# Issuing the transpose and the store of a query block's maxima one step later in a four-layer attention kernel

## The chip, the cores and the metric

The kernel runs on one core of one Trainium2 chip. The metric is the device time of one execution in microseconds (us). The engines are TensorE (PE for its matmuls, PEld for its weight loads), VectorE (DVE), ScalarE (ACT), GpSimd (POOL) and SyncE (SP), which issues every DMA of this kernel.

## The reference

Four residual layers, A, B, A, B, on x of 2048 tokens by 576 features, float32. Each layer normalizes x, does attention with 32 heads of 18 features and adds the projected result. In A every head has its own keys and values; in B all heads share one set.

```python
def _A_ref(x, wqkv, wo):
    qkv = (lambda x, *d: x.transpose(*d))((x @ wqkv).reshape(B, S, 3, H, Dh), 2, 0, 3, 1, 4)
    q, k, v = qkv[0], qkv[1], qkv[2]
    scores = jnp.einsum("bhqd,bhkd->bhqk", q, k) * (Dh ** -0.5)
    p = _softmax(scores, axis=-1)
    o = jnp.einsum("bhqk,bhkd->bhqd", p, v)
    return (lambda x, *d: x.transpose(*d))(o, 0, 2, 1, 3).reshape(B, S, D) @ wo
x = A_x
x = x + _A_ref(_layernorm(x, axis=-1), A_wqkv, A_wo)
x = x + _B_ref(_layernorm(x, axis=-1), B_wq, B_wk, B_wv, B_wo)
x = x + _A_ref(_layernorm(x, axis=-1), A_wqkv, A_wo)
x = x + _B_ref(_layernorm(x, axis=-1), B_wq, B_wk, B_wv, B_wo)
```

## The kernel before

Each layer projects q, k and v, then runs attention, then projects the output. Attention is cut into units: 16 pairs of heads `p` times 4 query blocks `u` of 512 queries, 64 units a layer and 256 in all. The two heads of a pair sit in the two row halves of TensorE, so two score matmuls can run side by side.

The scores of a unit are computed twice. The **max pass** (`max_mm`) lays queries on partitions: 32 tiles `psm` of 128 queries by 512 keys, each reduced to one maximum per query by VectorE (L615). For eight key blocks a difference tile `psd` goes through a Relu on ScalarE (L605) and is added to another tile before the maximum is taken (L612, the kinds `d` and `t`), which saves VectorE four tiles. The **exp pass** (`exp_mm`, L756) lays keys on partitions: 32 tiles `pse` of 128 keys by 512 queries, which ScalarE turns into `pt` or `side` (L762). `pv_block` (L783) multiplies these by the values into `oacc`. The `psm` tiles rotate through three PSUM banks, the `pse` and `psd` tiles through four, so a matmul waits until the reduction or the exponential of the tile three or four places before it has been read.

The maximum reaches the exponential through the matmul. When the 32nd max tile of a unit is reduced, `max_final` (L730) takes the negated maximum per query (`neg`, L732, VectorE) and splits it on GpSimd into a high and a low part (`hl`, L197 and L736). `max_store` (L738) transposes `hl` on VectorE (`tr`, L741) and issues four small DMAs that write it to DRAM (`m_d`, L743). `max_rows` (L745) issues two DMAs that read it back into two rows of the query operand `big` (L747), which face rows of ones in the keys. `exp_mm` of that unit reads these rows.

The order of the work is written out by hand. `UNIT` lists, for the two halves, `e` (an exp tile), `m`, `t` or `d` (a max tile); a number is so many columns of `pv_block`. While the exp tiles of one unit run, the max tiles of later ones run in between. The 32nd max tile of the next unit falls on the ninth word of the list.

```python
UNIT = """te ee 256 em me 384 et em me 512 et me ee 448 md dm em 384 em me 192 me ee me 192 md em 384
          me me em 384 em ee te 192 mm ee 384 dm em em 384 me"""
```

Everything else is hung on steps. A step is four exp tiles, a unit has `STEPS` = 8 of them, and `run_todo` is called before every word of the list with `LEAD + STEPS * w + sum(e_next) // 4`; it emits what is due. Instructions go to each engine's queue in the order in which they are emitted, and each queue is worked off in that order.

```python
b = STEPS * (4 * p + u) + STEPS - 1
if is_a or p or u:
    at(b + NM_AT, max_store, p, u)
    at(b + ROW_AT, max_rows, p, u)
for d, f in ((SUM_AT, o_sum), (L_AT, l_part), (INV_AT, l_inv), (R_AT, l_out), (RB_AT, l_rows),
             (MUL_AT, o_mul), (O_AT, o_out)):
    at(b + LEAD + d, f, p, u)
```

Counted from the start of the unit whose exp tiles run (w), the steps hold: step 2 `l_rows` of unit w-2; step 3 `o_sum` of w-1 and `max_store` of w+1; step 4 `o_mul` of w-2 and `l_part` of w-1, and in one unit of four `load_kd`; step 6 `o_out` of w-2 and `max_rows` of w+1; step 7 `l_inv` and `l_out` of w-1. Within a step the order is that of the calls of `at`, an earlier unit's before a later one's, `load_kd` last. `o_sum` and `o_mul` are GpSimd work on the sums (`os`, L197, L797, L819); `l_part` (L802), `l_out` (L809), `l_rows` (L814), `o_out` (L824) and `load_kd` (L486) issue DMAs.

Of the kernel before, what the change touches and what calls it, by code (L numbers as in the profile page):

```python
# [43 lines left out]

STEPS = 8
LEAD = 14
NM_AT = 2
ROW_AT = 5
SUM_AT = 4
L_AT = 5  # L50
# [72 lines left out]
def tile_kernel(ctx: ExitStack, tc: tile.TileContext, A_x, A_wqkv, A_wo, B_x, B_wq, B_wk, B_wv, B_wo, out):  # L123
# [291 lines left out]
    for layer in range(4):  # L415
# [412 lines left out]
        def at(b, f, *args):  # L828
            todo.setdefault(b, []).append((f, args))

        ns = STEPS * 4 * NPAIR
        for p in range(NPAIR):
            for u in range(4):
# [4 lines that stand above are left out]
# [93 lines left out]
```

## Time and profile before

| | before |
|---|---|
| median of 3 runs | 5737.49 us (5735.5 to 5739.29) |
| the profiled execution | 5738.74 us |
| its span | 5736.9 us |
| granted TensorE clock | 0.999 |
| units' distance in the steady part of a layer | 19.02 us |

The span runs from the first to the last instruction; the profiled execution's own time is 1.8 us more. An engine's busy time is the union of its instructions. TensorE's matmuls are pipelined and overlap, so its 99% is not 99% of what it could do; whether it waits is read from the starts of neighbouring matmuls. In the lists of instructions, a row gives the start in us from the span's start, the time from its first start to its last end, engine, line, operation, output and inputs, and how many were merged; in brackets stands the idle time before it and what ended that.

### The profile page before, as it was taken

How to read it: one execution, taken by the hardware profiler on the slowest of the kernel's cores; microseconds unless marked ns; L12 is line 12 of the kernel's file. 1: busy time of each engine (PE TensorE's matmuls, PEld its weight loads, DVE VectorE, ACT ScalarE, POOL GpSimd, SP SyncE). 2: the span in 40 equal slices, each digit the busy share in tenths (PEclk: the TensorE clock that was granted, in tenths of full speed). 3: DMA queues.
4: the chain of work that ended last, by engine and by line, in shares of the span. 5: the costliest groups of instructions: out<-in, count | busy, mean ns of one | idle time of the engine just before them, and what ended most of it. 6: DMA issues, size and time to landing. Idle time of an engine off the chain costs nothing.

```text
span 5736.9 us, 139041 instructions
## 1 busy us (share of the span) xinstructions
PE 5672.8 (99%) x53724; PEld 2800.5 (49%) x53724; DVE 4941.0 (86%) x9513; ACT 4951.8 (86%) x9868; POOL 1741.0 (30%) x2236
## 2 busy tenths in 40 slices
PE   9999999999999999999999999999999999999999
PEld 7644444444844444444685444444448444444446
DVE  5699999998699999999647999999977999999995
ACT  2599999999389999999625999999992899999996
POOL 3142323234233233333421332323342323323232
PEclk9999999999999999999999999999999999999999
DMA  6311111111320010000253111111114100000002
GB/s 224 114 45 38 35 38 35 38 36 25 125 67 23 23 23 20 22 21 24 59 191 94 49 36 37 38 36 39 33 31 134 53 23 24 23 23 20 23 14 78
DMA packets 258560, 291.64 MB, mean 51 GB/s; under 512 B 132700, under 2 KB 172892, under 8 KB 248176
## 3 DMA queue, kind: packets, MB, share of 16 engines
q1 hardware_dynamic: 257896, 282.75, 17.5%
q8 instruction: 422, 6.91, 0.5%
q14 instruction: 242, 1.98, 0.1%
HBM read 158.77 MB, written 119.86 MB: 49 GB/s over the span
## 4 chain that ended last, share of the span: by engine, by line
PE 74%; DVE 21%; POOL 2%; issue 1%; ACT 1%; DMA 0%; POOLq 0%; SPq 0%; DVEq 0%; ACTq 0%
PE oacc L783 26%; PE psm L608 18%; PE pse L756 16%; DVE mxd L615 13%; PE psn L275 6%; PE psq L434 6%; DVE side L612 6%; PE psd L600 2%; DVE tr L741 1%; POOL hl L736 1%; DVE neg L732 1%; POOL hl L197 1%; DVE mx L615 1%; PE ps L267 0%; POOLq L197 0%
## 5 line engine op out<-in xcount | busy, mean ns | idle before, releaser
L615 DVE TENSOR_REDUCE mxd<-psm 128x1 f32<-128x512 f32 x5856 | 3645.1, 681 | 129.8 <-PE pse L756 46.6
L762 ACT ACTIVATE pt<-pse 128x512 f32<-128x512 f32 x6580 | 3588.3, 622 | 110.6 <-PE pse L756 58.7
L608 PE MATMUL psm<-big 62*128 62x512 f32 x7216 | 2619.9, 453 | 30.6 <-DVE mx L615 5.0
L756 PE MATMUL pse<-big 64*128 64x512 f32 x8192 | 2465.5, 434 | 4.4 <-ACT pt L762 2.7
L783 PE MATMUL oacc<-pt,vbuf 128*19 128x64 f32 (+6 forms) x20492 | 1797.6, 377 | 3.8 <-DVE oc L197 3.6
L756 PEld LDWEIGHTS pse<-big 64*128 64x128 f32 x8192 | 1213.1, 185 | 904.8 <-ACT pt L762 538.3
L608 PEld LDWEIGHTS psm<-big 62*128 62x128 f32 x7216 | 1147.6, 184 | 807.4 <-DVE mxd L615 427.6
L783 PE MATMUL oacc<-side,vbuf 128*19 128x64 f32 (+6 forms) x5044 | 1408.5, 376 | 6.8 <-ACT side L762 6.8
L762 ACT ACTIVATE side<-pse 128x512 f32<-128x512 f32 x1612 | 999.9, 620 | 18.7 <-PE pse L756 7.1
L197 POOL TENSOR_SCALAR hl<-neg 128x8 fp32r<-128x8 f32 x256 | 50.6, 197 | 2854.6 <-DVE neg L732 2854.6
L783 PEld LDWEIGHTS oacc<-pt,vbuf 128*19 128x19 f32 x20492 | 454.2, 97 | 618.2 <-issue 504.7
L612 DVE CUSTOM_DVE_ANT_0 side<-psm,side 128x512 f32<-128x512 f32 x976 | 668.9, 685 | 36.5 <-PE psm L608 10.7
L605 ACT ACTIVATE side<-psd 128x512 f32<-128x512 f32 x976 | 591.6, 649 | 0.0
L783 PE MATMUL oacc<-pt,vy 128*19 128x384 f32 (+3 forms) x5756 | 587.6, 415 | 0.0
L806 POOL TENSOR_TENSOR rl<-lt,mone 128x8 f32<-128x8 f32 x256 | 422.9, 1652 | 358.2 <-DMA lt<-os 358.2
L783 PE MATMUL oacc<-side,vy 128*19 128x384 f32 (+2 forms) x1412 | 456.0, 414 | 0.0
L600 PE MATMUL psd<-kd,big 54*128 54x512 f32 x976 | 420.5, 471 | 0.0
L783 PEld LDWEIGHTS oacc<-side,vbuf 128*19 128x19 f32 x5044 | 319.8, 97 | 157.3 <-issue 124.6
L442 ACT ACTIVATE ev<-psq 128x512 fp32r<-128x512 f32 (+1 forms) x112 | 66.9, 598 | 325.9 <-PE psq L434 272.4
L819 POOL TENSOR_TENSOR os<-os,rb 96x512 f32<-96x512 f32 x256 | 327.7, 1280 | 20.6 <-DMA rb<-r_d 20.6
L797 POOL TENSOR_TENSOR os<-os,side 96x512 f32<-96x512 f32 x240 | 306.5, 1277 | 20.0
L197 POOL TENSOR_SCALAR os<-side 32x512 f32<-32x512 f32 x480 | 293.6, 612 | 40.0 <-POOL hl L736 0.2
(93 smaller groups left out, 3407.4 us busy)
## 6 DMA issues: line engine op xcount, KB each, us to landing
big<-qk_d SPq DMA_DIRECT2D x180, 432.0 KB
qk_d<-ev SPq DMA_DIRECT2D x96, 512.0 KB
qk_d<-ev SPq DMA_DIRECT2D x120, 256.0 KB
rb<-r_d SPq DMA_DIRECT2D x512, 36.0 KB
o_d<-os SPq DMA_DIRECT2D x512, 36.0 KB
m_d<-tr SPq DMA_DIRECT2D x1024, 2.0 KB
o<-o_d SPq DMA_DIRECT2D x64, 256.0 KB
big<-m_d SPq DMA_DIRECT2D x512, 4.0 KB
```

Of the source, the lines that this page charges most:

```text
L197: eng.tensor_scalar(dst, src, 1.0, 0.0, op0=OP.mult, op1=OP.add)
L275: nc.tensor.matmul(ps, lhs[:, xc, :], wsm[:, wc, h * 288:(h + 1) * 288], start=i == 0, stop=i == len(TERMS) - 1)
L434: nc.tensor.matmul(ps[:n].rearrange("p (u t) -> p u t", u=2)[:, us], w[:, wc, :n], xts[T][:, us, xc, :], start=(xc, wc) == TERMS[0], stop= ...
L600: nc.tensor.matmul(ps, q[b:b + 3 * DH, c0:c0 + P], kds[p if is_a else 0][b:b + 3 * DH], start=True, stop=True)
L605: nc.scalar.activation(r, ps, AF.Relu)
L608: nc.tensor.matmul(ps, q[b:b + KM, c0:c0 + P], k[b:b + KM, kb * 512:(kb + 1) * 512], start=True, stop=True)
L612: nc.vector.tensor_tensor_reduce(out=r, in0=ps, in1=r, scale=1.0, scalar=-3.0e38, op0=OP.add, op1=OP.max, accum_out=mx[:, r0:r0 + 1])
L615: nc.vector.reduce_max(mx[:, r0:r0 + 1], ps, axis=AX.X)
L756: nc.tensor.matmul(e, k[r:r + KE, kc * P:(kc + 1) * P], q[r:r + KE, u * 512:(u + 1) * 512], start=True, stop=True)
L762: nc.scalar.activation(pt, e, AF.Exp, scale=SCALE)
L783: nc.tensor.matmul(oacc[j:j + DH + 1, cs], v_of(kc)[:, 2 * p + a if is_a else 0, :], pts[p, u, i][:, cs], start=kc < 2 and c0 == 0, stop=k ...
L806: nc.gpsimd.tensor_tensor(rl, lts.pop((p, u)), mone, op=OP.pow)
```

## The change

`NM_AT` goes from 2 to 3. `max_store` of unit w+1 is emitted at step 4 of unit w where it was emitted at step 3. On VectorE the transpose then stands behind the reductions of the six max tiles in the words `md dm em em me me` (one of each word, `d` tiles go to ScalarE); on SP its four DMAs stand behind the two of `l_part`. `max_rows` stays at step 6. No instruction is added, removed or resized.

```diff
 STEPS = 8
 LEAD = 14
-NM_AT = 2
+NM_AT = 3
 ROW_AT = 5
 SUM_AT = 4
 L_AT = 5
```

## The prediction

> **What bounds the kernel now.** First the page: totals and the chain that ended last.
>
> ```profile
> span 5736.9 us, 139041 instructions
> ...
> PE 5672.8 (99%) x53724; PEld 2800.5 (49%) x53724; DVE 4941.0 (86%) x9513; ACT 4951.8 (86%) x9868; POOL 1741.0 (30%) x2236
> ...
> PE 74%; DVE 21%; POOL 2%; issue 1%; ACT 1%; DMA 0%; POOLq 0%; SPq 0%; DVEq 0%; ACTq 0%
> ```
>
> The chain lies on TensorE for three quarters and on VectorE for a fifth. GpSimd's 2% is odd for an engine that is idle 70% of the time: a GpSimd instruction is passed on the way. The list of waits says where, and the view of tile `tr` how often and how regularly the instruction runs.
>
> ```profile
> DVE tr L741 <- POOL hl L736: 152.4, 252, 0.6
> ...
> L741 DVE STREAM_TRANSPOSE tr<-hl x256: 200/211/215, 205.7 to 5644.3; 128x32 f32<-128x32 f32 x128
> ```
>
> In 252 of 256 units VectorE stands still for 152.4 / 252 = 0.605 us in front of the transpose until GpSimd has split the maxima. Whether that costs time is read from one unit: the chain in order of time, then VectorE's own list, around 804 us.
>
> ```profile
> 804.38 0.21 DVE tr L741
> 804.59 1.18 DVE mxd L615 x2
> 805.77 0.04 issue
> 805.81 0.49 PE psm L608
> ...
> 822.61 0.20 DVE neg L732
> ```
>
> ```profile
> 803.58 0.19 DVE L732 TENSOR_REDUCE neg<-mxd 128x8 f32<-128x32 f32 x1
> 804.38 0.21 DVE L741 STREAM_TRANSPOSE tr<-hl 128x32 f32<-128x32 f32 x1 [0.61 <-POOL hl L736]
> 804.51 5.43 DVE L615 TENSOR_REDUCE mxd<-psm 128x1 f32<-128x512 f32 x9
> 810.14 2.48 DVE L615 TENSOR_REDUCE mxd<-psm 128x1 f32<-128x512 f32 x4 [0.20 <-PE pse L756]
> ```
>
> The unit is 822.61 - 803.58 = 19.03 us long. The chain goes through the transpose and two reductions to the matmul at 805.81, and from there stays on TensorE until the next unit's reductions. After the transpose VectorE runs nine reductions without a break, 5.43 / 9 = 0.60 us each, and then waits again for TensorE. So it is late for a third of the unit only. TensorE's list tells what that costs; the first three rows are a place where it doesn't wait.
>
> ```profile
> 798.36 0.49 PE L756 MATMUL pse<-big 64*128 64x512 f32 x1
> ...
> 798.70 0.40 PE L756 MATMUL pse<-big 64*128 64x512 f32 x1
> 799.03 0.51 PE L783 MATMUL oacc<-pt,vy 128*19 128x384 f32 x3
> ...
> 803.45 0.50 PE L608 MATMUL psm<-big 62*128 62x512 f32 x1
> ...
> 805.20 0.50 PE L756 MATMUL pse<-big 64*128 64x512 f32 x1
> ...
> 805.81 0.49 PE L756 MATMUL pse<-big 64*128 64x512 f32 x1
> 806.24 0.34 PE L783 MATMUL oacc<-pt,vbuf 128*19 128x192 f32 x1
> ...
> 805.81 0.18 PEld L608 LDWEIGHTS psm<-big 62*128 62x128 f32 x1 [0.41 <-DVE mxd L615]
> ```
>
> Unhindered, a second pair of score matmuls starts 798.70 - 798.36 = 0.34 us after the first, and the value matmuls 799.03 - 798.70 = 0.33 us after that. Here it is 805.81 - 805.20 = 0.61 and 806.24 - 805.81 = 0.43. The weight load at 805.81 was let go by a reduction (that of the second tile after the transpose). So VectorE's lateness costs TensorE 0.61 - 0.34 = 0.27 us, and 0.10 us more because a weight load that waits can't run ahead: **0.37 us a unit**, not the 0.605 that VectorE stands.
>
> **The change part by part.** *VectorE's stall goes.* After `neg` the next instruction is now a reduction. Its tile is ready at 803.45 + 0.50 = 803.95; before, it started at 804.51. It can start up to 0.56 us earlier, and the second reduction, whose end lets the matmul go, with it: 805.77 - 0.56 = 805.21 at the earliest. TensorE wants that bank at 805.20 + 0.34 = 805.54, so it no longer waits as long as 0.23 of the 0.56 us are won. I take the whole 0.37.
>
> *The transpose at its new place.* Six reductions of 0.60 us after about 804.0 put it near 807.6. GpSimd's split was ready for the old place at 804.38, so nothing is waited for. It takes 804.51 - 804.38 = 0.13 us of VectorE's order. Just behind lies the 0.20 us idle time at 810.14, where VectorE waits for TensorE: the cover. VectorE itself runs 0.56 - 0.37 = 0.19 us further ahead of TensorE than now, so 0.20 + 0.19 - 0.13 leaves 0.26 us. I take nothing. Without the cover it would be 0.13 us x 252 = 33 us.
>
> *ScalarE.* It must follow a TensorE that is 0.37 us earlier.
>
> ```profile
> 804.27 1.14 ACT L605 ACTIVATE side<-psd 128x512 f32<-128x512 f32 x2
> ...
> 806.38 0.60 ACT L762 ACTIVATE side<-pse 128x512 f32<-128x512 f32 x1
> 807.26 2.06 ACT L762 ACTIVATE pt<-pse 128x512 f32<-128x512 f32 x4 [0.29 <-PE psm L608]
> ...
> 803.58:822.61 19.03, 18.93 (x194) 8.22 (x196) 17.70 (x34) 18.65 (x38) 5.79 (x7) 1.00 0.17 46
> ```
>
> The exponential at 806.38 started when its matmul ended (805.81 + 0.49 = 806.30), and the next one after 0.29 us of idle time, so ScalarE is waiting for the very matmuls that come earlier; it follows. But the last row (busy times of one unit: PE, PEld, DVE, ACT, POOL) leaves ScalarE only 19.03 - 18.65 = 0.38 us without any instruction. Overlap of neighbours makes that look tighter than it is: two L605 at 804.27 take 1.14 us together, four L762 at 807.26 take 2.06, so one more costs (2.06 - 1.14) / 2 = 0.46 us, and 37 tiles (32 exponentials, four Relu, one copy of `oacc`) cost 37 x 0.46 = 17.0 us. From both ends the reserve is 0.38 to 2.0 us; 0.37 fits into either. I cost it at nothing.
>
> *The DMAs.* SP's list of the same unit, then GpSimd's, then the first matmul that reads the rows:
>
> ```profile
> 804.62 1.69 SPq L743 DMA_DIRECT2D m_d<-tr  x4
> 807.12 1.14 SPq L802 DMA_DIRECT2D lt<-os  x2
> 808.37 0.80 SPq L486 DMA_DIRECT2D kd<-kd_d  x2
> 809.26 1.72 SPq L824 DMA_DIRECT2D o_d<-os  x2
> 811.08 0.54 SPq L747 DMA_DIRECT2D big<-m_d  x2
> 811.71 0.56 SPq L809 DMA_DIRECT2D r_d<-rl  x1
> ...
> 813.99 0.63 SPq L814 DMA_DIRECT2D rb<-r_d  x2
> ...
> 804.43 1.30 POOL L197 TENSOR_SCALAR os<-side 32x512 f32<-32x512 f32 x2
> ...
> 807.06 1.28 POOL L819 TENSOR_TENSOR os<-os,rb 96x512 f32<-96x512 f32 x1
> ...
> 816.17 0.71 PE L756 MATMUL pse<-big 64*128 64x512 f32 x3
> ```
>
> The four stores move from 804.62 behind `lt`: 807.12 + 1.14 = 808.3 (the transpose is done by 807.9). They end at 808.3 + 1.69 = 810.0. Behind them on SP come `kd` (one unit in four), `o_d` and the rows: 810.0 + 0.8 + 1.7 = 812.5. The rows also need the stores' data in DRAM. No row gives a landing; the nearest is the write `r_d`, issued by 811.71 + 0.56 = 812.27, whose reader `rb` starts at 813.99: 1.7 us. That gives 811.7, earlier than the queue. Rows issued by 812.5 + 0.54 = 813.1 and landed, with the same 1.7 us, at 814.8; lower end, with no landing time at all, 813.1. The first matmul that reads them is the three merged at 816.17, then at 815.80. Reserve: 1.0 to 2.7 us in this unit, which has all five issues, and 0.8 more where `kd` is missing. `r_d`, `rb` and the value sums behind them start 1.5 us later in the same way; `rb` is used by L819 in the next unit, at 807.06 + 19.03 = 826.1, ten us after its landing. I cost the queue at nothing.
>
> [...]
>
> *Sum.* 0.37 us x 252 units = 93 us. The profiled execution took 1.8 us beyond its span, 5738.7 us, and 1.25 us more than the median; 5737.5 - 93 = **5644 us**. Bounds of this case: only the wait itself, 0.27 us, is 68 us (5669); everything by which VectorE can come forward, 0.56 us, is 141 us (5596).
>
> **The rivals.** *VectorE's whole stall comes back* (a longer gain): 252 x 0.605 = 152 us, 5585 us. It would need further TensorE waits that come from the same lateness; the chain shows none after 805.81, which speaks against it.
>
> *ScalarE takes part of it back*: if its smallest reserve (0.38 us, all of it at the places where it is idle now) is used up by its own order, the unit shortens by about half of 0.37, say 0.18 us: 45 us, 5692 us. For it: ScalarE is as busy as VectorE. Against: it is idle exactly where the gain arises.
>
> *The transpose only stalls elsewhere.* At 807.6 GpSimd works on L819 (807.06 to 808.34). If the transpose had to wait for its end, VectorE would lose 0.7 us there, more than the 0.56 it won, the next reductions would be late again and TensorE would meet them in the following words: about no change, 5737 us. Against it: the transpose of 804.38 to 804.59 runs while GpSimd's L197 starts at 804.43, and its 256 durations lie between 200 and 215 ns. [...]
>
> *The rows come late* (slower). Place: the first exp matmul of each unit, at 815.80. It loses time as a whole once that matmul waits more than the 0.37 us won, that is, from rows landing after 816.2, 1.4 us behind my later bound. That happens if the four stores and the two reads, small and close together, each land 1.7 us later than `r_d` did: stores landed at 810.0 + 3.4 = 813.4, which now decides over the queue, rows issued by 813.9 and landed at 817.3, a wait of 1.5 us. If half of the units wait so (the others have the 0.8 us of `kd` in hand), the sum is 126 x 1.5 - 252 x 0.37 = +96 us, 5833 us. For it: both legs go through DRAM on one queue, and 3.7 us of the stores' lead are given away. Against: the reserve of 1.0 us and more.
>
> **How the numbers follow.** Forecast 0.62; whole stall 0.08; ScalarE 0.10; stalled elsewhere 0.07; rows late 0.13. A measurement of this kernel tells 0.2%, about 11 us, from no change. Faster: 0.62 + 0.08 + 0.10 = 0.80; same 0.07; slower 0.13. The range takes in the forecast's own bounds (5596 to 5669), the whole stall (5585) and ScalarE's case (5669 to about 5715): 5585 to 5715 holds 0.62 + 0.08 + 0.10 = 0.80.
>
> **What would show it.** Right: the wait of `tr` for `hl` is gone from the list of waits; after `neg` a reduction follows within 0.5 us; the pair at 805.81 follows its predecessor by 0.34; units are 18.65 us long; the stores start near 808.3 in this unit's time. Wrong: a wait of `pse` matmuls for `big<-m_d`; `tr` with an idle time before it; units still 19.0 us long with ScalarE on the chain.

## The result and the profile after

| | before | after |
|---|---|---|
| median | 5738.39 us (4 runs, 5735.5 to 5743.99) | 5650.07 us (4 runs, 5649.35 to 5651.2) |
| ratio, 95% interval | | 0.9845 (0.9828 to 0.9862) |
| span of the profiled execution | 5736.9 us | 5647.6 us |
| distance of units, median of the steady part | 19.02 us | 18.665 us |
| first reduction behind `neg`, median | 0.925 us | 0.407 us |

The kernel is 1.5% faster. The spans differ by 89.3 us, and (19.02 - 18.665) x 252 units = 89.5 us: the whole gain lies in the units.

The page of the changed kernel, its chain that ended last:

```profile
PE 98%; DVE 1%; ACT 1%; DMA 0%; issue 0%; SPq 0%; POOL 0%; DVEq 0%; ACTq 0%; POOLq 0%
PE oacc L783 38%; PE pse L756 23%; PE psm L608 21%; PE psn L275 6%; PE psq L434 6%; PE psd L600 3%; DVE mx L615 0%; PE ps L267 0%; ACT pt L762 0%; DMA raw<-in_A_wqkv_dram 0%; DMA qk_d<-ev 0%; PE oacc L268 0%; ACT ev L442 0%; DVE yx L261 0%; DVE xx L261 0%
```

VectorE's 21% and GpSimd's 2% have left the chain; it lies on TensorE from end to end. The view of tile `tr` after the change: how long the transpose runs (ns: least, median, most) and the wait in front of it (us, times):

```profile
L741 DVE STREAM_TRANSPOSE tr<-hl x256: 201/202/214, 208.6 to 5555.0; 128x32 f32<-128x32 f32 x128
...
  POOL hl L736: 2.5, 4
```

Of 252 waits and 152.4 us, 4 waits and 2.5 us are left. The lists of VectorE, TensorE and GpSimd in the unit that corresponds to the one shown of before (its `neg` at 792.21 instead of 803.58):

```profile
792.21 0.19 DVE L732 TENSOR_REDUCE neg<-mxd 128x8 f32<-128x32 f32 x1
792.62 3.68 DVE L615 TENSOR_REDUCE mxd<-psm 128x1 f32<-128x512 f32 x6 [0.23 <-PE psd L600]
796.22 0.20 DVE L741 STREAM_TRANSPOSE tr<-hl 128x32 f32<-128x32 f32 x1
796.34 4.55 DVE L615 TENSOR_REDUCE mxd<-psm 128x1 f32<-128x512 f32 x7
```

```profile
793.83 0.50 PE L756 MATMUL pse<-big 64*128 64x512 f32 x1
...
794.17 0.40 PE L756 MATMUL pse<-big 64*128 64x512 f32 x1
794.50 0.34 PE L783 MATMUL oacc<-pt,vbuf 128*19 128x192 f32 x1
...
795.68 1.28 POOL L819 TENSOR_TENSOR os<-os,rb 96x512 f32<-96x512 f32 x1
```

Behind `neg` VectorE now waits 0.23 us for TensorE, instead of 0.61 us for GpSimd, and the first reduction follows `neg` by 0.41 us. The pair of matmuls that came 0.61 us after its predecessor comes 794.17 - 793.83 = 0.34 us after it, the value matmuls 0.33 us later: the pace of the undisturbed place. The transpose runs without a wait, for 0.20 us, in the middle of GpSimd's L819.

SP's list of the same unit:

```profile
795.75 1.14 SPq L802 DMA_DIRECT2D lt<-os  x2
796.98 2.92 SPq L743 DMA_DIRECT2D m_d<-tr  x4
800.01 0.63 SPq L486 DMA_DIRECT2D kd<-kd_d  x2
800.74 0.62 SPq L824 DMA_DIRECT2D o_d<-os  x2
801.53 0.52 SPq L747 DMA_DIRECT2D big<-m_d  x2
```

The stores are issued 4.8 us behind `neg` (before: 1.0) and the rows 9.3 us (before: 7.5). The first matmul that reads the rows starts at 804.41, 2.4 us after their last issue has ended. The list of SP's own waits has a line that was small before (18.6 us, 6 times): SP now holds the rows back until the stores have landed.

```profile
SPq L747 <- DMA m_d<-tr: 84.3, 207, 3.5
```

### The profile page after: what moved, and what is told of

It reads as the page before. It is cut to its first block, busy times and chain, and to the rows that moved or that the text cites. A ratio compares the mean times of both kernels' runs of the same rounds, so it can differ in the third digit from the quotient of the medians.

```text
span 5647.6 us, 138977 instructions
## 1 busy us (share of the span) xinstructions
PE 5609.6 (99%) x53724; PEld 2845.4 (50%) x53724; DVE 4957.8 (88%) x9513; ACT 4930.6 (87%) x9868; POOL 1746.3 (31%) x2236
## 4 chain that ended last, share of the span: by engine, by line
PE 98%; DVE 1%; ACT 1%; DMA 0%; issue 0%; SPq 0%; POOL 0%; DVEq 0%; ACTq 0%; POOLq 0%
PE oacc L783 38%; PE pse L756 23%; PE psm L608 21%; PE psn L275 6%; PE psq L434 6%; PE psd L600 3%; DVE mx L615 0%; PE ps L267 0%; ACT pt L762 0%; DMA raw<-in_A_wqkv_dram 0%; DMA qk_d<-ev 0%; PE oacc L268 0%; ACT ev L442 0%; DVE yx L261 0%; DVE xx L261 0%
## 5 line engine op out<-in xcount | busy, mean ns | idle before, releaser
L615 DVE TENSOR_REDUCE mxd<-psm 128x1 f32<-128x512 f32 x5856 | 3689.1, 683 | 172.3 <-PE psd L600 60.0
L608 PE MATMUL psm<-big 62*128 62x512 f32 x7216 | 2524.8, 446 | 5.1 <-DVE mx L615 3.8
L756 PE MATMUL pse<-big 64*128 64x512 f32 x8192 | 2411.3, 431 | 4.2 <-ACT pt L762 2.5
L608 PEld LDWEIGHTS psm<-big 62*128 62x128 f32 x7216 | 1135.0, 184 | 705.4 <-DVE mxd L615 253.8
L819 POOL TENSOR_TENSOR os<-os,rb 96x512 f32<-96x512 f32 x256 | 328.6, 1284 | 19.9 <-DMA rb<-r_d 19.8
```

The source lines that it names most:

```text
L608: nc.tensor.matmul(ps, q[b:b + KM, c0:c0 + P], k[b:b + KM, kb * 512:(kb + 1) * 512], start=True, stop=True)
L615: nc.vector.reduce_max(mx[:, r0:r0 + 1], ps, axis=AX.X)
L756: nc.tensor.matmul(e, k[r:r + KE, kc * P:(kc + 1) * P], q[r:r + KE, u * 512:(u + 1) * 512], start=True, stop=True)
```

## The experiments

Three theories were set against each other: that TensorE paid for VectorE's lateness behind `neg`; that the gain comes from the stores' new place on SP; that only the wait for another engine costs, not VectorE's work. The costs that the prediction put at nothing (the transpose's new place, the queue) were measured too.

**Only the stores move** (`split`). The transpose is put back, its four DMAs stay late.

```diff
-NM_AT = 3
+NM_AT = 2
+ST_AT = 3
...
-at(b + NM_AT, max_store, p, u)
+at(b + NM_AT, max_tr, p, u)
+at(b + ST_AT, max_dma, p, u)
```

> The transpose goes back to step 3, behind the negated maximum; only its four stores stay at step 4, behind lt on SP. Theory (VectorE's lateness at the old place is what TensorE paid): the wait of tr for hl is back, 0.60 us in some 250 units, units are 19.02 us long, time 5737 us. Rival (the gain came from the stores' new place in SP's queue): units 18.66 us, time 5650 us.

Measured: 5740.89 us, ratio to before 1.0004 (0.9995 to 1.0013), units 19.02 us. The list of waits and SP's list:

```profile
DVE tr L744 <- POOL hl L739: 152.4, 252, 0.6
...
788.96 1.16 SPq L809 DMA_DIRECT2D lt<-os  x2
790.21 1.92 SPq L750 DMA_DIRECT2D m_d<-tr  x4
```

The stores stand behind `lt` as in the changed kernel, the wait is that of before to the tenth of a us, and the time is that of before (the interval of the ratio holds 1). The stores' place brings nothing and costs nothing.

**The transpose behind one reduction** (`one_reduce`). `max_store` is called right after the first VectorE reduction that follows `max_final` (the last unit of a layer, which has none, keeps step 4).

```diff
+if kind != "d" and ready_u:
+    max_store(*ready_u.pop())
 m_count[p, u] = m_count.get((p, u), 0) + 1
 if m_count[p, u] == 32:
     max_final(p, u)
+    if (is_a or p or u) and (p, u) != (NPAIR - 1, 3):
+        ready_u.append((p, u))
```

> Transpose and stores go out right after the first reduction behind the negated maximum instead of after the sixth. Theory: that reduction, 0.60 us and started 0.23 us after VectorE is free, covers GpSimd's split, so tr waits less than 0.1 us; its own 0.13 us fits into the 0.20 us by which the second reduction frees its bank before the matmul takes it; units 18.66 us, time 5650 us, with the stores some 3 us earlier than in the changed kernel. Rival (the stores' late place brings the gain): 5737 us.

Measured: 5650.43 us, ratio 0.9846 (0.9832 to 0.9861), units 18.667 us: the changed kernel's time. VectorE's and SP's lists:

```profile
773.81 0.19 DVE L737 TENSOR_REDUCE neg<-mxd 128x8 f32<-128x32 f32 x1
774.23 0.69 DVE L616 TENSOR_REDUCE mxd<-psm 128x1 f32<-128x512 f32 x1 [0.23 <-PE psd L601]
774.83 0.20 DVE L746 STREAM_TRANSPOSE tr<-hl 128x32 f32<-128x32 f32 x1
...
775.06 1.69 SPq L748 DMA_DIRECT2D m_d<-tr  x4
777.35 1.16 SPq L807 DMA_DIRECT2D lt<-os  x2
```

One reduction in between hides the split, and the stores go out 1.25 us behind `neg`, nearly as early as before. The order on VectorE makes the gain; one tile of distance is enough.

**Work instead of a wait at the old place** (`old_place_5`, `_3`, `_1`). The changed kernel with extra transposes of a constant tile, which nobody reads, at step 3.

```diff
+def extra(n):
+    for _ in range(n):
+        nc.vector.transpose(dum, zeros[:, :32])
...
+at(b + 2, extra, 5)
 at(b + NM_AT, max_store, p, u)
```

> The changed kernel with five extra 128x32 transposes of a constant tile, that nobody reads, at the old place (step 3). They wait for nothing and take 5 x 0.13 = 0.67 us of VectorE. Theory: VectorE's time at this place is what counts, worked or waited. Covered are 0.23 us of idle time there and the 0.20 us of slack of the second reduction; 0.24 us is left, and 0.10 us for the weight load: 0.34 us x 250 = 85 us, time 5735 us, units 19.0 us. Rival (only a wait for another engine costs, VectorE's work is hidden, it is busy 88%): 5650 us.

Measured: 5808.3 us, ratio 1.0122 (1.0107 to 1.0137), units 19.31 us. Work costs like a wait, but the size expected was wrong. VectorE's list says why:

```profile
791.03 0.19 DVE L733 TENSOR_REDUCE neg<-mxd 128x8 f32<-128x32 f32 x1
791.13 1.18 DVE L748 STREAM_TRANSPOSE dum<-zeros 128x32 f32<-128x32 f32 x5
792.24 3.64 DVE L616 TENSOR_REDUCE mxd<-psm 128x1 f32<-128x512 f32 x6
```

The five write one tile, each starts after the end of the one before, and they take 1.18 us, not 0.67, which had been worked out from the 0.13 us between a transpose and a reduction. The first reduction follows `neg` by 1.21 us. That led to two more runs, with the size worked out from this trace:

> The same with three extra transposes at the old place. In old_place_5 each took 0.246 us, not 0.13, since each waits for the one before it; its first reduction started 1.21 us behind the negated maximum, in the changed kernel 0.42, in the kernel before 0.93, and the units grew by 0.65 and 0.36 us against the changed kernel: in both the lateness less 0.16 us. With three the first reduction starts 0.10 + 3 x 0.246 - 0.11 = 0.73 us behind it, 0.31 us late: 0.31 - 0.16 = 0.15 us x 250 = 38 us, time 5688 us, units 18.82 us. If the extra instructions cost in proportion to their own time instead (0.65 us for five), three cost 0.39 us: 5748 us.

> The same with one extra transpose at the old place. The first reduction could start 0.24 us behind the negated maximum, but its tile is ready only at 0.42: covered, 5650 us, units 18.66 us. In proportion to its own time: 0.13 us a unit, 5683 us.

Measured: 5683.78 us with three (ratio 0.9899, 0.9881 to 0.9917) and 5644.48 us with one (0.9834, 0.9818 to 0.9849; its interval overlaps that of the changed kernel, and so it isn't called faster). Together, with medians over each trace:

| | first reduction behind `neg` | later than after | unit | longer than after | difference of the two |
|---|---|---|---|---|---|
| after | 0.407 us | 0 | 18.665 us | 0 | |
| one extra | 0.408 | 0.00 | 18.66 | 0.00 | |
| three extra | 0.721 | 0.31 | 18.82 | 0.155 | 0.16 |
| before | 0.925 | 0.52 | 19.02 | 0.355 | 0.16 |
| five extra | 1.213 | 0.81 | 19.31 | 0.645 | 0.16 |

Whether the lateness is waited or worked, the unit pays all of it but 0.16 us. That this is the slack of the second tile's bank is argued, not shown: in the changed kernel the second reduction behind `neg` ends at 793.91, and the matmul that takes its bank starts 0.26 us later, at 794.17. The rivals fall: work isn't hidden, and it doesn't cost by its own length either, since one extra transpose is free.

**The cover at the new place** (`new_place_2`): two of the same transposes in front of the moved one.

```diff
+at(b + NM_AT, extra, 2)
 at(b + NM_AT, max_store, p, u)
```

> The changed kernel with two extra 128x32 transposes of a constant tile in front of the moved one: 0.27 us of VectorE at the new place. By the prediction's cover of 0.26 us that costs nothing: 5650 us. By the trace of the changed kernel the third reduction behind the transpose frees its bank only 0.13 us before a matmul takes it: 0.14 us late, and about 0.10 us for the weight load, 0.24 us x 250 = 60 us: 5710 us.

Measured: 5734.11 us, ratio 0.999 (0.998 to 0.9999), units 19.005 us. VectorE's list, in which the last reduction before the transposes starts at 787.56:

```profile
788.16 0.45 DVE L748 STREAM_TRANSPOSE dum<-zeros 128x32 f32<-128x32 f32 x2
788.60 0.21 DVE L742 STREAM_TRANSPOSE tr<-hl 128x32 f32<-128x32 f32 x1
788.74 4.36 DVE L616 TENSOR_REDUCE mxd<-psm 128x1 f32<-128x512 f32 x7
```

From that reduction to the next it takes 1.18 us, in the changed kernel 0.72 (795.62 to 796.34): 0.46 us more, of which the unit pays 19.005 - 18.665 = 0.34. The cover is 0.12 us. Neither expected time came; both had taken the two transposes at 0.27 us, and they take 0.46. The second, 5710 us, had the right mechanism. A bank sets the cover, not VectorE's idle time: in the changed kernel the third reduction behind the transpose ends at 798.26, and the matmul that takes its bank starts at 798.44. In this run the third reduction ends at 790.58, and the weight load of that matmul is let go by it:

```profile
790.63 0.18 PEld L609 LDWEIGHTS psm<-big 62*128 62x128 f32 x1 [0.28 <-DVE mxd L616]
```

From the reduction's end to the load it takes 0.05 us. That leaves 798.44 - 798.26 - 0.05 = 0.13 us in the changed kernel, which fits the cover.

**The rows' reserve** (`nm_4`, `nm_5`): `NM_AT` 4, then 5.

```diff
-NM_AT = 3
+NM_AT = 4
```

> Transpose and stores one step later still (step 5), behind three more reductions, 1.9 us. Theory: the rows then are issued by about 2 us before the first exp matmul of their unit (the changed kernel has 1.7 to 4 us), which is still enough; the transpose stands where VectorE waits 0.2 us anyway: units 18.66 us, time 5650 us. Rival (the rows' reserve is used up already): a wait of the exp matmuls for the rows, each us of it 250 us: 5700 us and more.

> Transpose, stores and reading of the rows all in step 6, the stores straight before the reads on SP. Worked out from the changed kernel's trace: stores issued by 10.1 us after the negated maximum, reads 1.06 us later, all issued about 0.5 us before the first exp matmul wants the rows. With the landing of 1.06 us that the stores show or of 1.7 us as for r_d, each unit waits 0.55 to 1.2 us: 5790 to 5950 us, with a wait of TensorE for big<-m_d. If the rows land within 0.5 us of their issue: 5650 us.

Measured for `nm_4`: 5654.48 us, ratio 0.9849 (0.9833 to 0.9865), units 18.66 us; eight units are 18.9 to 19.6 us long (in the changed kernel one is, with 18.9). In one of the eight the chain goes through the landing of the stores, 3.66 us from 1631.42, and that of the rows, 1.41 us from 1635.37, to the first matmul that reads them. For `nm_5`: 6070.9 us, ratio 1.0581 (1.0565 to 1.0596), outside the range expected, which was too low. The list of waits of `nm_5`, its chain in order of time in one unit, and two stretches of the table of stretches (columns: length, busy time of PE, PEld, DVE, ACT, POOL, granted TensorE clock, DMA share, GB/s):

```profile
PE pse L756 <- DMA big<-m_d: 266.8, 243, 2.7
```

```profile
845.46 0.21 DVE tr L741
...
846.96 1.40 DMA m_d<-tr
...
848.51 0.23 SPq L747
848.73 0.04 issue
848.78 1.33 DMA big<-m_d
850.11 0.14 issue
850.24 0.70 PE pse L756 x3
```

```profile
820.00:826.00 6.00, 4.88 (x51) 2.23 (x47) 5.80 (x12) 5.20 (x11) 0.00 (x0) 1.00 0.03 4
826.00:834.00 8.00, 6.38 (x41) 2.63 (x45) 2.27 (x7) 3.54 (x7) 0.00 (x0) 0.58 0.23 67
```

Now the rival of the prediction is there: TensorE waits for the rows in 243 units, 266.8 / 243 = 1.1 us each. The chain shows what no row of before had shown, the landing: 1.40 us from the start of the last store's issue, 1.33 us from that of the second read's. The expected 0.55 to 1.2 us a unit was right for the wait, the unit of 19.9 us (median) is 1.24 us longer; but that makes 1.24 x 252 = 312 us of the 421 us by which the span grew beyond the changed kernel's. The rest lies in longer units, about two thirds of it in 28 units of 21.7 to 24.6 us, in which clock was lost: between 826 and 834 us, for instance, the granted clock is 0.58; a wait of 2.7 us stands there, from 824.9 to 827.6. Some 46 units of 20.2 to 22.5 us kept the full clock.

## Why the prediction was right

- **What bounds the kernel**: right. TensorE paid for VectorE's lateness behind `neg` and for nothing else of the step; `split` and the table of the extra transposes show both halves.
- **0.37 us a unit**: 0.355 measured. The wait of 0.27 and the weight load's 0.10 were read from starts of matmuls and are both gone (0.34 and 0.33 us where 0.61 and 0.43 stood). The first reduction comes forward by 0.52 of the 0.56 us allowed. That 0.23 of the 0.56 us would be enough was wrong: by the table all of the 0.52 but 0.16 us, 0.36 us, has to be won, and with three extra transposes, where 0.20 us is won, 0.155 us a unit is still paid. The 0.23 was counted from the matmul's wait alone and left out the weight load's 0.10. The change wins enough by either count. 93 us were forecast, 88 to 89 came: the difference is 0.015 us x 252 = 4 us.
- **The whole stall of 0.605 us doesn't come back**: right. 0.16 us of the lateness had always been covered, and TensorE is on the chain with 98% as soon as VectorE is out of the way. That share alone proves little: it is 98% with three extra transposes too, where each unit still pays 0.155 us.
- **The transpose's new place**: that it costs nothing was right, the reason was not sized right. The step "leaves 0.26 us" counted the idle time that VectorE reaches later; `new_place_2` shows 0.12 us, since the banks of the tiles in between are wanted before that. More than half of the cover was not there. The view of `tr` puts 76.3 us of idle time in front of 241 weight loads down to the moved transpose; they cost nothing, since `one_reduce`, where the view lists none, has the same units.
- **No stall at the new place**: the transpose runs 0.20 us, within L819 (795.68 to 796.96), and doesn't wait for its end: in the changed kernel its duration lies between 201 and 214 ns in all 256 units, and in 228 of them it runs wholly inside one GpSimd instruction.
- **ScalarE follows**: right; it is on 1% of the chain, as before.
- **The DMAs**: the stores' issue was forecast 808.3 - 803.58 = 4.7 us behind `neg` and came at 4.8; the end of the rows' issue at 9.5 and 9.8. The landing was taken as 1.7 us after the last issue's end and was 850.11 - (848.51 + 0.53) = 1.07 in `nm_5`. With that the rows of the unit shown land at 802.05 + 1.07 = 803.1, 1.3 us before 804.41; forecast were 1.0 to 2.7. The prediction had the stores' landing earlier than the queue; in 207 of 256 units SP waits for it, 84.3 / 207 = 0.41 us each, and the reserve holds all the same. From issue to landing the chain shows 1.33 and 1.40 us for these small DMAs of SyncE in the unit of `nm_5` shown, and 3.66 us for the stores in that of `nm_4`. `nm_4` shows the reserve from the other side: one more step, and eight units grow longer.

## What to carry to other kernels

In these runs an instruction that waits for another engine didn't cost the wait but the lateness of what stands behind it in its queue, less a slack of 0.16 us, most likely that of the first buffer that someone else wants back; read that slack from the starts of the consumer, not from the producer's idle time. One independent piece of work between the request and the use was enough here, a reduction of 0.60 us, and the earliest place that has it leaves the largest reserve for the transfers behind. Before a step is moved later, the time from its last DMA's landing to the first reader is the budget; beyond it the price here was nearly five times the gain (421 us against 89).

## What the runs showed of the hardware

- Small transposes that write the same tile one behind the other start 0.246 us apart in `old_place_5` (791.13, then four more in 1.18 us), and in `new_place_2` a transpose into another tile starts 0.21 us behind (788.39 and 788.60), when the one before has ended; so the common tile isn't the whole reason. A reduction starts 0.13 us behind a transpose (804.38 and 804.51 in the kernel before).
- In `nm_5`, whose mean granted clock was 0.987 (0.998 in the changed kernel), TensorE lost clock in 28 of the 70 units in which it waited 1.2 to 2.7 us for the rows, and, away from the start of a layer, in no unit with a shorter wait; in the one with the wait of 2.7 us 0.58 was granted between 826 and 834 us, and the unit was 24.6 us long. In the other 42 the clock stayed full after waits of up to 2.5 us, so the length of the wait doesn't decide it alone.
